# First down product in blocks of 512 tokens, and the second layer's weight combinations formed one product later

## The chip, the core and the metric

The kernel runs on one core of a Trainium2 chip. The metric is the device time of one execution in microseconds (us), compared as medians of runs on the same chip.

## What is computed

Attention with 32 packed queries per head (batch 8, 8 heads, 576 positions, head size 64) feeds two layers of the same shape (4608 tokens, model width 512, inner width 2048):

```python
p_packed = sm_attn(p, k, v)
x = sm_attn(q, p_packed, p_packed)        # then tokens x 512
h = x @ w_in;  y = (h * cos(h)) @ w_out                 # first layer
h = y @ w_in2; out = where(h >= 1, h, where(h <= -1, 0, (h + 1)**2 / 4)) @ w_out2
```

## The kernel before

All matmuls are float32 products in three terms: each operand is split into a rounded part and a remainder (`split`: one ScalarE copy at L67, one subtraction at L68), and `TERMS` names the three pairs that are multiplied. The weights arrive as 64-bit floats; `convert` rebuilds 32-bit values from their two words (L132 on ScalarE, then L134, L135, L138, L139 and L142 on VectorE).

The program has four stages, one after the other:

- **Front**: attention for batch n beside the first up product. `up(n, hf, fp)` is one item: 12 matmuls of 288 columns (L616), a copy `u` out of PSUM (L623 or L625) and a store of 288 KB to the scratch tensor `h1T`. There are 128 items, and beside each the streams of generators (`load`, `wt`, `wo`, `frm`, `mat`, `att`) are advanced by one step. The stream `wo` converts and splits `w_out` in 16 slices over the last 32 items (`cut_w_out`).
- **First down product** (`run_down1`): 16 blocks of 288 tokens, 8 items each. An item loads 288 KB of `h1T`, forms h*cos(h) (`act_a`: L789 and L790; `act_b`: L797 and L798), splits it into a tile `r1` (`part`), and multiplies it with `w_out` in 24 matmuls of 288 columns (L824). Loads run 7 items ahead in 8 buffers; `r1` has 4 buffers.
- **Second up product** (`run_up2`): 8 batches, 4 pairs of slices each, seven products (`ORDER_UP`) of 12 matmuls per pair (L745), since this layer multiplies 2 x 2 blocks with seven products in place of eight.
- **Second down product** (`run_down2`): again seven products per batch (L928).

The seven products need sums and differences of the weight blocks. `combine` forms them in units, as the stream `wt`: a unit loads 1 MB (two loads at L545), converts it, forms four combinations (L570 to L573), splits them, and stores seven pieces of 256 KB (L552) to `su` (for the up product, 8 units) or `sd` (for the down product, 8 units). The tiles of `su` and `sd` are read back by the loads at L668. A unit has one raw tile; its second half `hl` receives the split parts and must be stored before the next pair is written to it.

Instructions stand in a fixed order on each engine and each engine takes them in that order. The order was set by a scheduler when the program was built, from the order of the code and from what each instruction needs; memory that a pool takes over from a closed pool makes its first writers wait for the last readers. Before the change, the 8 units of `su` start in the middle of the front, in the pool `late` on the right side of memory; the pool of `r1` is opened on the same side after `late` is closed.

Of the kernel before, what the change touches and what calls it, by code (L numbers as in the profile page):

```python
# [9 lines left out]
F32 = mybir.dt.float32  # L10
# [17 lines left out]
def body(ctx: ExitStack, tc: tile.TileContext, q, k, v, p, w_in, w_out, w_in2, w_out2, out):  # L28
# [25 lines left out]
    h1T = dram.tile([NFT // 2, 128, NT // HB, 2, HB], F32, name="h1T")  # L54
# [486 lines left out]
    def combine(units):  # L541
        def load(src):
            raw = prep[0].tile([128, 4, 256, 2], I32, tag="raw", name="raw")
            for x in range(2):
                nc.sync.dma_start(out=raw[:, 2 * x:2 * x + 2], in_=src(x))  # L545
            return raw

        held = []

        def store():  # L550
            for dst, x in held:
                nc.sync.dma_start(out=dst, in_=x)  # L552
            held.clear()

        units = list(units)
        raw = load(units[0][0])
        yield
        for u, (_, dst) in enumerate(units):

            a = prep[0].tile([128, 4, 256], F32, tag="pa", name="pa")  # L560
            convert(raw, a, last_act)
            store()
            yield
            s, hl = (
                raw[:, 2 * i:2 * i + 2].rearrange("p m c t -> p (m c t)") for i in range(2)
            )
            s = s.bitcast(F32).rearrange("p (k c) -> p k c", c=256)
            hl = hl.bitcast(F32R).rearrange("p (l n c) -> p l n c", l=2, n=2)
            tt = nc.vector.tensor_tensor
            tt(out=s[:, 0], in0=a[:, 1], in1=a[:, 3], op=ALU.add)  # L570
            tt(out=s[:, 2], in0=a[:, 0], in1=a[:, 1], op=ALU.subtract)
            tt(out=s[:, 1], in0=s[:, 0], in1=a[:, 0], op=ALU.subtract)
            tt(out=s[:, 3], in0=a[:, 2], in1=s[:, 1], op=ALU.subtract)  # L573
            yield
            for k, n in ((0, 2), (2, 1), (3, 2), (5, 2)):
                x = {0: a[:, 0:4:2], 2: a[:, 3:4], 3: s[:, :2], 5: s[:, 2:]}[k]
                with behind(last_act):
                    split(hl[:, 0, :n], hl[:, 1, :n], x, nc.vector)
# [26 lines left out]
    def up(n, hf, fp):  # L605
# [20 lines left out]
        late_store(h1T[fp, :, 2 * n + hf], u)  # L626
# [83 lines left out]
    def bank(x):  # L710
        return ps2.tile([128, 2, 512], F32, tag=x, name="ps" + x, bufs=2 if x == "Z" else 1)[:, :, :HB]
# [58 lines left out]

    def load_h1(i):
        if i < B * 16:
            t = dn1["g"].tile([128, 2, HB], F32, tag="g", name="h1")
            nc.sync.dma_start(out=t, in_=h1T[i % 8, :, i // 8])
            G1[i] = t

    def run_down1():
        po = pd.enter_context(tc.tile_pool(name="dn_o", bufs=3, reuse_waits="tile"))
# [4 lines left out]
        streams["wt"].append(combine(list(units_down())[:4]))  # L783

        def act_a(i):
            if i < B * 16:
                t = turns[i] = pt.tile([128, 2, HB], F32, tag="t", name="t")
                ki = t.bitcast(I32)
                nc.scalar.activation(out=ki, in_=G1[i], func=AF.Copy, scale=1 / (2 * PI), bias=0.25)  # L789
                nc.vector.scalar_tensor_tensor(  # L790
                    out=t, in0=G1[i], scalar=1 / (2 * PI), in1=ki, op0=ALU.mult, op1=ALU.subtract
                )

        def act_b(i):
            if i < B * 16:
# [4 lines left out]
        def part(i):  # L800
            if i < B * 16:
                r = parts[i] = dn1["r"].tile([128, 2, 2, HB], F32R, tag="r", name="r1")
                split(r[:, 0], r[:, 1], turns.pop(i), nc.vector)
# [6 lines left out]
        for i in range(B * 16):  # L810
            blk, c = divmod(i, 8)
            if c == 0:
                acc = [bank("Z") for _ in range(2)] if blk % 2 else [bank(x) for x in "XY"]
            load_h1(i + 7)
# [4 lines left out]
            for k in range(2):  # L819
                f = 2 * c + k  # L820
                for d in range(NDT):
                    ds = slice(d * 128, d * 128 + 128)
                    for n, (w, y) in enumerate(TERMS):
                        nc.tensor.matmul(  # L824
# [3 lines left out]
            if c == 7:  # L828
                for j in range(2):
                    y = po.tile([128, 2, HB], F32, tag="o", name="o1")  # L830
# [4 lines left out]
                    late_store(  # L835
                        yT[j * 256:j * 256 + 256, blk * HB:blk * HB + HB].rearrange("(j p) t -> p j t", p=128), y
# [3 lines left out]
            if i % 4 == 2:  # L840
                step("wt")
            if i == 13 * 8:
                drain("wt")
                for o in ORDER_UP[:6]:
                    load_su(0, o)
# [6 lines left out]
    def run_up2():  # L852
# [12 lines left out]
        streams["wt"].append(combine(list(units_down())[4:]))  # L865
        last = None
        for p in range(B):
            for f in range(0, 8, 2):
# [4 lines left out]
                for o in ORDER_UP[:6]:  # L873
                    product_up(p, f, o, st)
                    if o[0] == "X":
# [113 lines left out]
    for i, (n, hf, fp) in enumerate(items):  # L989
# [9 lines left out]
        if i == n_first + 1:  # L999
# [4 lines left out]
            prep[:] = late  # L1004
            streams["wt"].append(combine(units_up()))
# [6 lines left out]
        if n == B - 1 and hf and fp == 0:  # L1012
# [73 lines left out]
```

## Time and profile before

| | |
|---|---|
| median of 3 runs | 1780.81 us (1777.97 to 1781.54) |
| the profiled execution | 1794.1 us, its span 1792.2 us |
| TensorE busy (PE) | 1582.3 us, 88% of the span |
| VectorE busy (DVE) | 1222.4 us, 68% |
| ScalarE busy (ACT) | 944.7 us, 53% |
| GpSimd busy (POOL) | 231.0 us, 13% |
| mean granted TensorE clock | 0.928 of full speed |
| moved by DMA | 333.24 MB, mean 186 GB/s |

The span runs from the first to the last instruction. TensorE is busy for most of it, but the shares differ by stage: in two stretches it is far from full, the front (0 to about 515 us) and the end of the front (515 to 603 us).

### The profile page before, as it was taken

The numbers are of one execution on the slowest core, as the hardware profiler recorded it, in microseconds if no ns is written. First come the engines' busy times: TensorE is split into PE (matmuls) and PEld (weight loads), VectorE is DVE, ScalarE is ACT, GpSimd is POOL, SyncE is SP. The second block draws the span as 40 slices with busy tenths as digits, with TensorE's granted clock in tenths as the row PEclk, the third lists the DMA queues.
The fourth block names the chain that finished last, engine by engine and source line by source line (L and its number), as shares of the span: only waits on it lengthen the run. The fifth ranks groups of instructions, "written<-read, shape, count | busy, mean of one in ns | idle before, by whom it ended". The sixth has DMA issues, their size and how long they took to land.

```text
span 1792.2 us, 28398 instructions
## 1 busy us (share of the span) xinstructions
PE 1582.3 (88%) x10846; PEld 1521.1 (85%) x10846; DVE 1222.4 (68%) x1787; ACT 944.7 (53%) x1530; POOL 231.0 (13%) x154
## 2 busy tenths in 40 slices
PE   9579988988830598999999999899999899999998
PEld 7459876878730598999999999889999899999998
DVE  6873345658763688887677467886666587777774
ACT  4353444545432466676666456667667444444443
POOL 0221001222000001000000213444442000000000
PEclk7779988989875799999999999999999999999999
DMA  7666889998785375554344555543334964444430
GB/s 254 162 184 211 242 295 278 303 300 300 267 281 178 99 214 160 182 164 119 108 120 117 200 200 191 177 159 132 131 133 178 396 198 133 133 133 133 133 107 34
DMA packets 177994, 333.24 MB, mean 186 GB/s; under 512 B 16576, under 2 KB 70848, under 8 KB 174272
## 3 DMA queue, kind: packets, MB, share of 16 engines
q1 hardware_dynamic: 123584, 237.02, 43.1%
q10 hardware_dynamic: 54272, 94.39, 14.1%
q8 instruction: 85, 1.39, 0.3%
q14 instruction: 53, 0.43, 0.1%
HBM read 190.84 MB, written 136.31 MB: 183 GB/s over the span
## 4 chain that ended last, share of the span: by engine, by line
PE 62%; DMA 19%; DVE 12%; issue 3%; ACT 3%; SPq 1%; ACTq 0%; DVEq 0%
PE psZ L928 9%; PE psZ L824 8%; PE hps L616 7%; PE psZ L745 6%; PE psY L928 5%; PE psX L928 5%; PE psY L745 4%; PE psX L745 4%; PE psX L824 4%; PE psY L824 4%; DMA sd<-raw 3%; DMA su<-raw 3%; DMA raw<-in_moe_w_in 3%; DMA raw<-in_moe_w_out 2%; PE psA L279 2%
## 5 line engine op out<-in xcount | busy, mean ns | idle before, releaser
L616 PE MATMUL hps<-at,m 128*128 128x288 f32 x1536 | 251.7, 321 | 33.9 <-ACT u L625 22.4
L616 PEld LDWEIGHTS hps<-at,m 128*128 128x128 f32 x1536 | 231.7, 206 | 48.1 <-ACT u L625 26.0
L67 ACT ACTIVATE r<-g 128x576 fp32r<-128x576 f32 x224 | 153.5, 686 | 180.7 <-PE psZ L928 71.6
L68 DVE TENSOR_TENSOR r<-g,r 128x576 fp32r<-128x576 f32 x224 | 166.3, 754 | 69.3 <-ACT r L67 69.1
L824 PE MATMUL psZ<-r,wo 128*128 128x288 f32 x1536 | 207.9, 296 | 4.4 <-DVE r L68 2.2
L824 PEld LDWEIGHTS psZ<-r,wo 128*128 128x128 f32 x1536 | 205.6, 188 | 6.0 <-DVE r L68 3.3
L824 PE MATMUL psX<-r,wo 128*128 128x288 f32 x768 | 126.2, 300 | 90.5 <-ACT r L67 87.6
L824 PEld LDWEIGHTS psX<-r,wo 128*128 128x128 f32 x768 | 111.4, 191 | 91.4 <-ACT r L67 87.9
L928 PE MATMUL psZ<-r,sw 128*128 128x288 f32 x1152 | 158.2, 296 | 1.6 <-DVE o L723 0.9
L928 PEld LDWEIGHTS psZ<-r,sw 128*128 128x128 f32 x1152 | 155.0, 188 | 2.0 <-issue 1.1
L731 DVE SCALAR_TENSOR_TENSOR t<-hh,t 128x576 f32<-128x576 f32 x128 | 117.6, 921 | 42.0 <-ACT t L730 41.5
L68 DVE TENSOR_TENSOR r<-t,r 128x576 fp32r<-128x576 f32 x128 | 99.1, 777 | 58.6 <-ACT r L67 58.4
L729 ACT ACTIVATE t<-hh,half 128x576 f32<-128x576 f32 x128 | 98.5, 772 | 57.2 <-DVE hh L723 46.5
L824 PE MATMUL psY<-r,wo 128*128 128x288 f32 x768 | 125.5, 299 | 0.0
L67 ACT ACTIVATE r<-t 128x576 fp32r<-128x576 f32 x128 | 86.9, 681 | 66.2 <-PE psZ L824 32.5
L68 POOL TENSOR_TENSOR ty<-td,ty 128x576 fp32r<-128x576 f32 x32 | 53.8, 1687 | 523.0 <-ACT ty L67 523.0
L745 PE MATMUL psZ<-ty,sw 128*128 128x288 f32 x768 | 112.8, 297 | 7.2 <-DVE hh L723 6.9
L928 PE MATMUL psX<-r,sm 128*128 128x288 f32 x768 | 108.2, 301 | 10.0 <-ACT r L67 9.8
L928 PEld LDWEIGHTS psX<-r,sm 128*128 128x128 f32 x768 | 106.0, 193 | 10.6 <-ACT r L67 10.1
L745 PEld LDWEIGHTS psZ<-ty,sw 128*128 128x128 f32 x768 | 105.6, 188 | 8.5 <-DVE hh L723 8.0
L824 PEld LDWEIGHTS psY<-r,wo 128*128 128x128 f32 x768 | 111.5, 191 | 0.0
L797 ACT ACTIVATE t<-t,halfpi 128x576 f32<-128x576 f32 x128 | 97.5, 767 | 14.1 <-DVE t L790 13.9
(160 smaller groups left out, 2820.0 us busy)
## 6 DMA issues: line engine op xcount, KB each, us to landing
h1T<-u ACTq DMA_DIRECT2D x128, 288.0 KB, 4.2
h<-h1T SPq DMA_DIRECT2D x128, 288.0 KB, 2.9
gT<-t ACTq DMA_DIRECT2D x128, 288.0 KB, 2.1
g<-gT SPq DMA_DIRECT2D x128, 288.0 KB, 3.2
raw<-in_moe_w_in SPq DMA_DIRECT2D x32, 512.0 KB, 5.7
raw<-in_moe_w_out SPq DMA_DIRECT2D x32, 512.0 KB, 5.4
su<-raw SPq DMA_DIRECT2D x56, 256.0 KB, 3.4
sd<-raw SPq DMA_DIRECT2D x56, 256.0 KB, 2.9
```

Source lines behind the costliest of these rows:

```text
L67: nc.scalar.activation(out=hi, in_=src, func=AF.Copy)
L68: (eng or nc.gpsimd).tensor_tensor(out=lo, in0=src, in1=hi.bitcast(F32), op=ALU.subtract)
L279: nc.tensor.matmul(out=pp[:, s * 64:s * 64 + 64], lhsT=ve[:, s * 128:s * 128 + 128], rhs=e[:, pos * 64:pos * 64 + 64], start=(c == 0), sto ...
L616: nc.tensor.matmul(out=hps[:, j, :HB], lhsT=m[:, w, G, cs], rhs=x[:, G, y], start=(G == 0 and i == 0), stop=(G == 1 and i == 2),)
L729: nc.scalar.activation(out=t, in_=h, func=AF.Relu, scale=0.5, bias=half)
L731: nc.vector.scalar_tensor_tensor(out=t, in0=h, scalar=1.0, in1=t, op0=ALU.max, op1=ALU.min)
L745: nc.tensor.matmul(out=ps[:, i], lhsT=s[:, d, w, cs], rhs=t[:, d, y], start=first and d == n == 0, stop=d == 1 and n == 2, skip_group_chec ...
L797: nc.scalar.activation(out=t, in_=t, func=AF.Sin, scale=2 * PI, bias=halfpi)
L824: nc.tensor.matmul(out=acc[d // 2][:, d % 2], lhsT=wo[f // 4, w][:, f % 4, ds], rhs=r[:, y, k], start=f == n == 0, stop=f == NFT - 1 and n ...
L928: nc.tensor.matmul(out=ps[:, j], lhsT=s[:, f % 4, w, j * 128:j * 128 + 128], rhs=r[:, y, k], start=first and f == n == 0, stop=f == 7 and ...
```

## The change

The first down product works in 9 blocks of 512 tokens: an item loads 512 KB, and its 24 matmuls have 512 columns; 72 items in place of 128. `h1T` is laid out so that a row of tokens is contiguous, so each store of `u` goes out in two pieces of 1152 bytes per partition in place of one of 2304. Its buffers are fewer and larger: 4 for the loads (3 items ahead in place of 7), 2 for `r1`, 2 for the output. The 8 units of `su` are advanced in the first down product, one step per item, and no longer in the front; all 8 units of `sd` are advanced in the second up product, three steps per pair in place of two. Split parts alternate between the raw tile and a new tile `pl`, so the wait for a store is for the one before the last. Six loads of `su` are wrapped in `issue_after` a matmul.

```diff
-    h1T = dram.tile([NFT // 2, 128, NT // HB, 2, HB], F32, name="h1T")
+    h1T = dram.tile([NFT // 2, 128, 2, NT], F32, name="h1T")
...
-            hl = hl.bitcast(F32R).rearrange("p (l n c) -> p l n c", l=2, n=2)
+            hls = [hl.bitcast(F32R).rearrange("p (l n c) -> p l n c", l=2, n=2),
+                   prep[0].tile([128, 2, 2, 256], F32R, tag="pl", name="pl")]
...
-            for k, n in ((0, 2), (2, 1), (3, 2), (5, 2)):
+            for j, (k, n) in enumerate(((0, 2), (2, 1), (3, 2), (5, 2))):
+                hl = hls[j % 2]
...
-        late_store(h1T[fp, :, 2 * n + hf], u)
+        t0 = n * S + hf * HB
+        late_store(h1T[fp, :, :, t0:t0 + HB], u)
...
+    n_items = NT // 512 * 8
...
-            t = dn1["g"].tile([128, 2, HB], F32, tag="g", name="h1")
-            nc.sync.dma_start(out=t, in_=h1T[i % 8, :, i // 8])
+            t = dn1["g"].tile([128, 2, 512], F32, tag="g", name="h1")
+            nc.sync.dma_start(out=t, in_=h1T[i % 8][:, :, i // 8 * 512:i // 8 * 512 + 512])
...
-        streams["wt"].append(combine(list(units_down())[:4]))
+        streams["wt"].append(combine(units_up()))
+        last_act.clear()
...
-            load_h1(i + 7)
+            load_h1(i + 3)
...
-            if i % 4 == 2:
+            if True:
                 step("wt")
-            if i == 13 * 8:
+            if i == 7 * 8:
                 drain("wt")
-                for o in ORDER_UP[:6]:
-                    load_su(0, o)
+                with tc.issue_after(mm.ins):
+                    for o in ORDER_UP[:6]:
+                        load_su(0, o)
...
-        streams["wt"].append(combine(list(units_down())[4:]))
+        streams["wt"].append(combine(units_down()))
...
-                    if o[0] == "X":
+                    if o in ("X1", "X2", "Y5"):
                         step("wt")
...
-            prep[:] = late
-            streams["wt"].append(combine(units_up()))
...
-            dn1["g"] = pd.enter_context(tc.tile_pool(name="dn_g", bufs=8, reuse_waits="tile", side="right"))
-            dn1["r"] = pd.enter_context(tc.tile_pool(name="dn_r", bufs=4, reuse_waits="tile", side="right"))
-            for j in range(7):
+            dn1["g"] = pd.enter_context(tc.tile_pool(name="dn_g", bufs=4, reuse_waits="tile", side="right"))
+            dn1["r"] = pd.enter_context(tc.tile_pool(name="dn_r", bufs=2, reuse_waits="tile", side="right"))
+            for j in range(3):
                 load_h1(j)
```

How the order on the engines moves is shown at two places. The first is VectorE's queue at the end of the front. Before, from the last slice of `w_out` (`wo`) to the subtractions of the first tiles `r_...` of the first down product; two whole units (`pa`, `raw`) stand between them, of which the second is the block from L134 to L68:

```order
L68 TENSOR_TENSOR wo<-w_4548,wo 128x512
...
L68 TENSOR_TENSOR raw<-raw 128x512 x2
L134 TENSOR_SCALAR pa<-raw 128x1024
L135 SCALAR_TENSOR_TENSOR pa<-raw,pa 128x1024
L138 TENSOR_SCALAR raw<-pa 128x1024
L139 SCALAR_TENSOR_TENSOR raw<-raw 128x1024
L142 TENSOR_TENSOR pa<-pa,raw 128x1024
...
L68 TENSOR_TENSOR raw<-raw 128x512 x2
L68 TENSOR_TENSOR r_4764<-t,r_4764 128x576
L68 TENSOR_TENSOR r_4771<-t,r_4771 128x576
```

After the change, the same queue from the last slice of `w_out` to the first tile `r_4524`:

```order
L68 TENSOR_TENSOR wo<-w_4316,wo 128x512
L134 TENSOR_SCALAR pa<-raw 128x1024
L135 SCALAR_TENSOR_TENSOR pa<-raw,pa 128x1024
L796 SCALAR_TENSOR_TENSOR t<-h_4361,t 128x1024
L138 TENSOR_SCALAR raw<-pa 128x1024
L796 SCALAR_TENSOR_TENSOR t<-h_4363,t 128x1024
L139 SCALAR_TENSOR_TENSOR raw<-raw 128x1024
L804 TENSOR_TENSOR t<-h_4361,t 128x1024
L796 SCALAR_TENSOR_TENSOR t<-h_4365,t 128x1024
L142 TENSOR_TENSOR pa<-pa,raw 128x1024
L796 SCALAR_TENSOR_TENSOR t<-h_4529,t 128x1024
L804 TENSOR_TENSOR t<-h_4363,t 128x1024
```

The next row is the subtraction of `r_4524`. In place of two whole units, the conversion of one unit (the fourth) and seven operations of the first items now stand ahead of the first `r` tile; three units have gone before, and four follow in the product.

The second place is SyncE's queue, which issues the loads, at the start of the first down product after the change. `h_...` are the loads of items 0 to 6 and on, `sm` the loads of `su` (L671) that `issue_after` encloses in the code:

```order
L552 DMA su<-pl 128x2x256 x2
L545 DMA raw<-in_moe_w_in 128x2x512 x2
L779 DMA h_4361<-h1T 128x2x512
...
L779 DMA h_4682<-h1T 128x2x512
L671 DMA sm<-su 128x2048
L552 DMA su<-raw 128x2x256 x2
...
L545 DMA raw<-in_moe_w_in 128x2x512
L671 DMA sm<-su 128x2048 x5
L779 DMA h_4795<-h1T 128x2x512
```

The stores of the third unit and the raw loads of the fourth stand ahead of the first item's load, and the six loads of `su` stand around the loads of items 8 to 10, not at item 56 where the code has them: `issue_after` binds instructions of the matmul's own engine, and these are issued by SyncE. Before, the same six loads stood among the loads of `w_out` at the end of the front.

## Rows read from the trace of the kernel before

**Rows 1.** The page: busy tenths and granted clock in 40 slices of 44.8 us.

```profile
PE   9579988988830598999999999899999899999998
PEclk7779988989875799999999999999999999999999
```

**Rows 2.** TensorE's waits, 602 to 1013 us: total, times, longest.

```profile
PE psX L824 <- ACT r L67: 87.6, 1, 87.6
```

**Rows 3.** Timeline at the end of the front: start, us, instructions, idle before.

```profile
511.74 3.54 PE L616 MATMUL hps<-at,m 128*128 128x288 f32 x24 [0.23 <-ACT u L625]
516.87 0.63 ACT L67 ACTIVATE wo<-w 128x512 fp32r<-128x512 f32 x1 [1.96 <-DVE w L142]
...
540.71 0.63 ACT L67 ACTIVATE wo<-w 128x512 fp32r<-128x512 f32 x1 [2.24 <-DVE w L142]
541.51 1.21 SPq L545 DMA_DIRECT2D raw<-in_moe_w_in  x2
549.89 1.10 ACT L132 ACTIVATE raw<-raw 128x1024 f32<-128x1024 f32 x1 [8.56 <-DMA raw<-in_moe_w_in]
...
576.92 1.21 SPq L545 DMA_DIRECT2D raw<-in_moe_w_in  x2
583.20 1.10 ACT L132 ACTIVATE raw<-raw 128x1024 f32<-128x1024 f32 x1 [9.95 <-DMA raw<-in_moe_w_in]
...
602.17 2.40 ACT L67 ACTIVATE r<-t 128x576 fp32r<-128x576 f32 x4
```

**Rows 4.** Chain that ended last, 330 to 545 us: its pieces on units' transfers.

```profile
370.48 6.68 DMA su<-raw
...
383.87 7.84 DMA raw<-in_moe_w_in
...
425.97 5.88 DMA su<-raw
...
432.58 8.77 DMA raw<-in_moe_w_in
...
474.45 8.64 DMA su<-raw
```

**Rows 5.** Windows: busy us of PE, PEld, DVE, ACT, POOL (instructions); clock, DMA share, GB/s.

```profile
400.00:500.00 100.00, 81.76 (x513) 77.74 (x513) 79.94 (x123) 47.55 (x78) 14.74 (x9) 0.89 0.85 286
...
542.00:603.00 61.00, 0.11 (x1) 0.11 (x1) 22.87 (x36) 14.02 (x21) 0.00 (x0) 0.50 0.45 144
```

**Rows 6.** TensorE's timeline: runs of matmuls of 288 and of 512 columns.

```profile
360.88 0.86 PE L426 MATMUL psD<-wi,mt 128*128 128x512 f32 x3
361.58 1.49 PE L616 MATMUL hps<-at,m 128*128 128x288 f32 x10
...
631.42 25.76 PE L824 MATMUL psZ<-r,wo 128*128 128x288 f32 x192
657.02 0.96 PE L824 MATMUL psX<-r,wo 128*128 128x288 f32 x6
```

**Rows 7.** TensorE's timeline: first matmuls of the two middle products.

```profile
602.89 0.61 PE L824 MATMUL psX<-r,wo 128*128 128x288 f32 x1 [87.62 <-ACT r L67]
...
1026.47 1.77 PE L745 MATMUL psX<-ty,sm 128*128 128x288 f32 x12
```

**Rows 8.** Groups by shape: count, busy, mean ns of one, idle before.

```profile
L135 DVE SCALAR_TENSOR_TENSOR pa<-raw,pa 128x1024 int32<-128x1024 int32 x16 | 20.8, 1300 | 0.1
L142 DVE TENSOR_TENSOR pa<-pa,raw 128x1024 f32<-128x1024 f32 x16 | 20.7, 1291 | 0.1
```

**Rows 9.** TensorE's timeline in the second up product: all four stalls beside units.

```profile
1083.13 3.14 PE L745 MATMUL psY<-ty,sm 128*128 128x288 f32 x12 [1.97 <-DVE hh L723]
1121.48 1.87 PE L745 MATMUL psX<-ty,sw 128*128 128x288 f32 x12 [1.38 <-ACT p L718]
1132.82 1.86 PE L745 MATMUL psZ<-ty,sw 128*128 128x288 f32 x12 [3.07 <-DVE hh L723]
1137.80 3.19 PE L745 MATMUL psY<-ty,sm 128*128 128x288 f32 x12 [3.13 <-DVE hh L723]
```

**Rows 10.** DMA issues: count, KB each, median us to landing.

```profile
h1T<-u ACTq DMA_DIRECT2D x128, 288.0 KB, 4.2
h<-h1T SPq DMA_DIRECT2D x128, 288.0 KB, 2.9
yT<-o ACTq DMA_DIRECT2D x32, 288.0 KB, 2.9
sm<-su SPq DMA_DIRECT2D x6, 1024.0 KB, 7.6
```

More of the change, by code (lines that the diff above doesn't have):

```diff
@@ L708, in load_y, with bank @@
         tile_of("Z4", diff(b21, t2, t2))
-    def bank(x):
-        return ps2.tile([128, 2, 512], F32, tag=x, name="ps" + x, bufs=2 if x == "Z" else 1)[:, :, :HB]
+    def bank(x, n=HB):
+        return ps2.tile([128, 2, 512], F32, tag=x, name="ps" + x, bufs=2 if x == "Z" else 1)[:, :, :n]
     def wtile(pool, tag, bufs):
@@ L769, in body @@
     G1 = {}
+    n_items = NT // 512 * 8
     def load_h1(i):
-        if i < B * 16:
-            t = dn1["g"].tile([128, 2, HB], F32, tag="g", name="h1")
-            nc.sync.dma_start(out=t, in_=h1T[i % 8, :, i // 8])
+        if i < n_items:
+            t = dn1["g"].tile([128, 2, 512], F32, tag="g", name="h1")
+            nc.sync.dma_start(out=t, in_=h1T[i % 8][:, :, i // 8 * 512:i // 8 * 512 + 512])
             G1[i] = t
     def run_down1():
-        po = pd.enter_context(tc.tile_pool(name="dn_o", bufs=3, reuse_waits="tile"))
+        po = pd.enter_context(tc.tile_pool(name="dn_o", bufs=2, reuse_waits="tile"))
         pt = pd.enter_context(tc.tile_pool(name="dn_t", bufs=4, reuse_waits="tile"))
@@ L782, in run_down1 @@
         prep[:] = [pd.enter_context(tc.tile_pool(name="prep1", bufs=1, reuse_waits="tile"))]
-        streams["wt"].append(combine(list(units_down())[:4]))
+        streams["wt"].append(combine(units_up()))
+        last_act.clear()
         def act_a(i):
-            if i < B * 16:
-                t = turns[i] = pt.tile([128, 2, HB], F32, tag="t", name="t")
+            if i < n_items:
+                t = turns[i] = pt.tile([128, 2, 512], F32, tag="t", name="t")
                 ki = t.bitcast(I32)
@@ L794, in act_b @@
         def act_b(i):
-            if i < B * 16:
+            if i < n_items:
                 t = turns[i]
@@ L800, in part @@
         def part(i):
-            if i < B * 16:
-                r = parts[i] = dn1["r"].tile([128, 2, 2, HB], F32R, tag="r", name="r1")
+            if i < n_items:
+                r = parts[i] = dn1["r"].tile([128, 2, 2, 512], F32R, tag="r", name="r1")
                 split(r[:, 0], r[:, 1], turns.pop(i), nc.vector)
@@ L809, in run_down1 @@
         part(0)
-        for i in range(B * 16):
+        for i in range(n_items):
             blk, c = divmod(i, 8)
             if c == 0:
-                acc = [bank("Z") for _ in range(2)] if blk % 2 else [bank(x) for x in "XY"]
-            load_h1(i + 7)
+                acc = [bank("Z", 512) for _ in range(2)] if blk % 2 else [bank(x, 512) for x in "XY"]
+            load_h1(i + 3)
             part(i + 1)
@@ L823, in run_down1 @@
                     for n, (w, y) in enumerate(TERMS):
-                        nc.tensor.matmul(
+                        mm = nc.tensor.matmul(
                             out=acc[d // 2][:, d % 2], lhsT=wo[f // 4, w][:, f % 4, ds], rhs=r[:, y, k],
@@ L829, in run_down1 @@
                 for j in range(2):
-                    y = po.tile([128, 2, HB], F32, tag="o", name="o1")
+                    y = po.tile([128, 2, 512], F32, tag="o", name="o1")
                     if j:
@@ L835, in run_down1 @@
                     late_store(
-                        yT[j * 256:j * 256 + 256, blk * HB:blk * HB + HB].rearrange("(j p) t -> p j t", p=128), y
+                        yT[j * 256:j * 256 + 256, blk * 512:blk * 512 + 512].rearrange("(j p) t -> p j t", p=128), y
                     )
```

## The prediction

> **What bounds the kernel now.** I read the page first. TensorE's row of slices [rows 1] shows a front that is mostly full, a hole at its end, and products that fill nearly everything from the fifteenth slice on. In the hole, the twelfth to fourteenth slices, the digits are 3, 0, 5, and the granted clock falls to 0.5 of full speed, its lower level. The waits of TensorE in the first down product [rows 2] name it: one wait of 87.6 us for ScalarE's copy into `r`. The timeline [rows 3] shows what happens inside: the last matmuls of the front end at 515.3, slices of `w_out` are finished until 541.3, and then two units of `su` run alone, one after the other, with their loads issued at 541.51 and 576.92. Only at 602.17 does `r` get written, and the product starts at 602.89 [rows 7]. `r` comes after both because its pool takes over memory of the units' pool `late`. Elsewhere units lie beside matmuls; these two lie beside nothing.
>
> In the front itself, the chain of waits runs through units too: five transfers of units make up 37.8 us of it between 370 and 483 [rows 4]. VectorE is busy 80% and the DMA engines 85% there, while TensorE's 513 matmuls of that window, at the pace worked out next, would fit in 68 of its 100 us [rows 5]. After that, the first down product runs without gaps: it takes 1026.47 - 602.89 = 423.6 us [rows 7], and 192 matmuls take 657.02 - 631.42 = 25.6 us, 0.1333 us each [rows 6], so its 3072 matmuls are 409.6 us and 14.0 us are start and small waits. TensorE is the bound of everything from 603 us on.
>
> **The change part by part.** All terms are in us of the profiled execution (1794.1, a span of 1792.2); it lies 13.3 above the median of 1780.81, and I carry the sum over to that median as it is.
>
> *Front, until its last up matmul.* Before, five units and the load of a sixth lie ahead of this point; after, two units do, late in the front. What can be won is bounded by the 37.8 us of unit transfers on the chain. Not all of it comes back: when one piece leaves a chain, the next-latest takes over, here `h1T` stores and slices of `w_out`, and two units remain. I take 22, a little over half; ends 5 and 40. The two-piece stores of `h1T` I cost at nothing: stores of `yT` already go out in pieces of 1152 bytes and land in 2.9 us at the median, against 4.2 for those of `h1T` [rows 10].
>
> *From the last up matmul to the first down matmul.* Before: 87.6. After, VectorE's and ScalarE's queues hold these steps ahead of the first `r`. Six slices of `w_out` follow the last up copy, the first half done: between 516.87 and 540.71 four intervals of slices took 23.84 us, 5.96 each [rows 3], so five of them are 29.8. The third unit stands between them. Its VectorE time comes from the window with two units and eight tile operations of 576 columns: an operation of 1024 takes 1.29 [rows 8], so one of 576 about 0.73, and (22.87 - 5.8)/2 = 8.5 us [rows 5]; I cost it at nothing, since a slice has six VectorE operations of 512 columns, which at half the durations of [rows 8] are under 4 of its 5.96 us, and at 8.5 if that cover fails. Then the third unit's last store must land before the raw tile is loaded again (about 3 us, as the stores of `yT` [rows 10]), the load takes 8.4 or 6.3 from issue to L132 [rows 3], mean 7.3, and L132 itself 1.1. L132 of the fourth unit stands ahead of the first item on ScalarE, so this wait is paid in full. Then VectorE has eleven rows and the subtraction of `r`: ten at 1.29 and two at about half, 14.2. Sum 29.8 + 3 + 7.3 + 1.1 + 14.2 = 55.4, a gain of 32. If slices and load overlap better it is 45, with the third unit uncovered 64: gains of 43 and 24. The two units that ran alone are not gone; they lie beside matmuls now.
>
> *The product itself.* 1728 matmuls of 512 columns. The front has such matmuls in runs of three: from 360.88 to 361.58 three starts, 0.2333 each [rows 6]. 1728 x 0.2333 = 403.2, a gain of 6.4 over 409.6. Bounds by the 288-column row: if its price is proportional to columns, 0.237 each and no gain; if the 0.0133 above 288 columns at 2.4 GHz is a fixed price per matmul, 0.2267 each, 391.7, a gain of 17.9. I take the measured run of three.
>
> The Trainium skill ("TensorE: Matmul & The Clock Gate", section "Back-to-back issue gap") gives N/2.4 plus 2.5 ns as the spacing of single matmuls, by which 512 columns would be an estimate of 215.8 ns and the product 372.9 us. The trace does not agree for 288 columns, 133.3 ns against the formula's 122.5, so I do not use it for the sum.
>
> Does VectorE keep up? An item needs three operations of 1.29, 3.9 us, against 24 x 0.2333 = 5.6 on TensorE. The units stand in the queue one per six to seven items: 6.5 x 3.9 + 8.5 = 33.8 against 36.4 us. It fits, with little room. With two `r` buffers ScalarE's copy for item i+1 waits for the end of item i-1 and then has one item, 5.6 us, for copy and subtraction (about 2.4) and what stands between; that is enough, but an item that also carries a conversion has 2 to 3 us of slack, not more. The `issue_after` does nothing for the `su` loads, which SyncE issues: five 1 MB loads go out ahead of item 10's load. At 7.6 us per landing [rows 10] for one, and a lead of three items or 16.8 us, I expect a wait of 2 us once; the ends are 0 and 10.
>
> *Second up product.* Twice as many units. The four before made TensorE wait 1.97 + 1.38 + 3.07 + 3.13 = 9.6 us, and after two of these waits twelve matmuls took 3.14 and 3.19 in place of 1.77 [rows 7, 9], 3.0 more with the other two: 12.6, or 3.1 per unit. Four more units at that price are 12.6. The tile `pl` takes some waits for stores off ScalarE, so I take 9; ends 0 and 25. The eighth unit's stores stand ahead of the last batch but one, so the second down product does not wait for `sd`.
>
> Sum: -22 - 32 - 6.4 + 2 + 9 = -49. Profiled 1745, median **1732**.
>
> **The rivals.**
>
> *The front frees more.* If the DMA engines were its true bound (85% busy at 286 GB/s, [rows 5]), three units fewer move 9 MB less, some 31 us at that rate, and the rest of the chain shortens too: 40 and 43 in place of 22 and 32, so -78, 1702. Against it: TensorE and VectorE stand on that chain as well.
>
> *The front hardly moves.* Slices of `w_out` pace its last 32 items at about 6 us per slice or more, units or not; then 5 and 24, and 12.6 for the units later: -20, 1760. For it: slices are spread over those items and wait for their loads.
>
> *512 columns at full rate.* In an unbroken run the price above the columns could vanish: 512/2.4 GHz is 0.2133, 368.6 in all, 34.6 more, 1697. Against it stands the unbroken run of 288 columns, at 0.1333 and not 0.12. (By the formula of the Trainium skill's page above it would be 30 more.)
>
> *Slower than before: the loads starve the product.* Three items of lead in place of seven, with stores and 1 MB loads ahead in SyncE's queue, each of which waits for VectorE. If every item waits, the gain of 49 is gone from 49/72 = 0.68 us per item on; at 1.5 us it ends at 1840. A tile of this sort lands in 2.9 us [rows 10] against a lead of 16.8, which speaks against it.
>
> *The change does not do what it says*: true of `issue_after`, whose price is in the sum.
>
> **How the numbers follow.** Forecast as summed 0.55 (1715 to 1748), more freed 0.17, hardly moved 0.17, full rate 0.04, starved 0.05, and 0.02 for gains and losses that cancel. A change of under 0.2%, 3.6 us, cannot be told from none. All but the last two are faster: 0.93, within 0.02, slower 0.05. The range from 1700 to 1763 leaves out the starved case, the full-rate case, nearly half of the "more freed" case and a little at the top.
>
> **What would show it.** Right: TensorE's wait ahead of the first down matmul falls from 87.6 to 45 to 64 us; the last up matmul ends between 475 and 510; 192 of the new matmuls take 44.8 us; the down product takes 405 to 422; stalls beside units in the second up product come to 15 to 30 in all. Wrong: waits for `h` loads in the down product, matmuls there with gaps at every item, a second up product more than 25 us longer than before, or a front that ends no earlier than 513.

## The result and the profile after

The changed kernel takes 1735.16 us at the median of 4 runs (1732.49 to 1736.27), the kernel before 1780.62 (1777.97 to 1781.54): a ratio of 0.9745, interval 0.9728 to 0.9762, or 45.5 us less. The forecast was 1732. The profiled execution took 1735.4 us, a span of 1733.6, so it stands for the median; that of the kernel before lay 13.5 above its own.

TensorE's slices on the page of the changed kernel, 43.3 us each, and the clock granted in them:

```profile
PE   9579998998816999999999889899999799999998
PEclk7769998999867999999999899999999899999999
```

Against [rows 1] the hole is most of the twelfth slice and a part of the thirteenth. The 0.6 there is a mean that takes in busy time; inside the hole, from 505 to 533, the granted clock is 0.50 as before. TensorE's timeline answers [rows 3, 6, 7]: the last up matmuls, the first of the first down product, one uninterrupted run of 192, the first of the second up product and of the second down product.

```profile
481.62 1.85 PE L618 MATMUL hps<-at,m 128*128 128x288 f32 x12 [0.77 <-ACT u L627]
533.85 0.79 PE L830 MATMUL psX<-r,wo 128*128 128x512 f32 x1 [50.37 <-ACT r L67]
...
584.47 44.96 PE L830 MATMUL psZ<-r,wo 128*128 128x512 f32 x192
629.27 0.39 PE L830 MATMUL psX<-r,wo 128*128 128x512 f32 x1
...
954.57 1.76 PE L748 MATMUL psX<-ty,sm 128*128 128x288 f32 x12
...
1353.55 2.70 PE L935 MATMUL psX<-r,sm 128*128 128x288 f32 x19
```

The end of the front is the start of the first down matmul less its wait: 483.5, against 515.3. Reading such rows for every kernel gives the table to which all that follows refers. Each row of it is one profiled execution; the last column reaches to the end of the span. "Move" is the move of the combinations, "blocks" are those of 512 tokens.

| kernel | median us | front ends | wait | first down | second up | rest |
|---|---|---|---|---|---|---|
| before, profile of 1794.1 | 1780.6 | 515.3 | 87.6 | 423.6 | 384.1 | 381.6 |
| before again, 1781.55 | | 509.1 | 85.4 | 422.6 | 382.7 | 380.0 |
| changed | 1735.2 | 483.5 | 50.4 | 420.7 | 399.0 | 380.0 |
| blocks alone | 1798.0 | 514.8 | 94.5 | 420.0 | 387.5 | 380.6 |
| move alone | 1710.2 | 473.9 | 33.7 | 424.4 | 397.3 | 379.4 |
| move, h1T in two pieces | 1712.2 | 469.1 | 34.1 | 428.3 | 395.4 | 380.3 |
| changed, no `pl` | 1734.0 | 481.0 | 40.4 | 428.8 | 398.8 | 379.0 |
| changed, units held | 1705.6 | 474.0 | 26.5 | 426.5 | 400.1 | 380.9 |
| changed, `su` loads held | 1730.1 | 479.3 | 50.8 | 421.4 | 402.3 | 380.5 |
| move, units held | 1699.9 | 472.4 | 27.2 | 425.5 | 390.8 | 379.5 |
| the same, first load held | 1705.0 | 468.1 | 23.8 | 428.4 | 405.2 | 379.4 |
| the same, ten units and six | 1699.5 | 472.9 | 23.0 | 432.5 | 392.5 | 380.4 |
| move, held, GpSimd added | 1727.7 | 475.9 | 27.4 | 448.8 | 394.6 | 379.2 |
| the same, 4 columns | 1706.3 | 473.4 | 26.6 | 430.5 | 395.3 | 379.3 |

Where blocks are of 512 tokens, 24 matmuls of the second up product (3.2 us) lie ahead of the end of the first down product (25 and 26 without `pl` and with the units held), so that its own time is 3.2 less than in the table, and the second up product's 3.2 more. The kernels ran on several chips, on which the kernel before had medians of 1780.6 to 1785.8; where two kernels on different chips differ by about 5 us, their ratios to it are what counts.

What fills the wait of 50.4 us shows in the timelines of SyncE and ScalarE, which answer [rows 3]: loads of the units' raw tiles, the last slice of `w_out`, the fourth unit's conversion (L132), and the first `r`. The last two rows, of VectorE and TensorE, are the subtraction of the same `r` and the matmuls that wait for it.

```profile
410.99 1.27 SPq L545 DMA_DIRECT2D raw<-in_moe_w_in  x2
450.58 1.46 SPq L545 DMA_DIRECT2D raw<-in_moe_w_in  x2
485.47 0.56 SPq L545 DMA_DIRECT2D raw<-in_moe_w_in  x1
...
514.88 0.63 ACT L67 ACTIVATE wo<-w 128x512 fp32r<-128x512 f32 x1 [2.33 <-DVE w L142]
515.56 1.21 SPq L545 DMA_DIRECT2D raw<-in_moe_w_in  x2
523.82 1.10 ACT L132 ACTIVATE raw<-raw 128x1024 f32<-128x1024 f32 x1 [8.32 <-DMA raw<-in_moe_w_in]
...
532.75 1.04 ACT L67 ACTIVATE r<-t 128x1024 fp32r<-128x1024 f32 x1
...
536.51 1.22 DVE L68 TENSOR_TENSOR r<-t,r 128x1024 fp32r<-128x1024 f32 x1
...
537.79 2.50 PE L830 MATMUL psX<-r,wo 128*128 128x512 f32 x5 [2.72 <-DVE r L68]
```

Two units lie wholly in the front, the third beside the last slices, and ScalarE then waits 8.32 us for the fourth's load, as the forecast had it. In the second up product TensorE's timeline has 21 waits where the kernel before has eight (four of them are [rows 9]); the longest of them, the first being that for the product's first tiles:

```profile
964.84 3.25 PE L748 MATMUL psX<-ty,sm 128*128 128x288 f32 x12 [6.91 <-ACT p L721]
...
1019.40 1.87 PE L748 MATMUL psY<-ty,sm 128*128 128x288 f32 x12 [2.28 <-DVE hh L726]
...
1122.10 1.87 PE L748 MATMUL psY<-ty,sm 128*128 128x288 f32 x12 [2.56 <-DVE hh L726]
...
1219.73 2.89 PE L748 MATMUL psZ<-ty,sw 128*128 128x288 f32 x12 [3.22 <-DVE hh L726]
```

### The profile page after: what moved, and what is told of

It is laid out like the page before. It is cut to its first block, busy times and chain, and to the rows that moved or that the text cites. A ratio compares the mean times of both kernels' runs of the same rounds, so it can differ in the third digit from the quotient of the medians.

```text
span 1733.6 us, 25137 instructions
## 1 busy us (share of the span) xinstructions
PE 1566.0 (90%) x9502; PEld 1422.9 (82%) x9502; DVE 1211.8 (70%) x1612; ACT 913.7 (53%) x1355; POOL 232.2 (13%) x154
## 4 chain that ended last, share of the span: by engine, by line
PE 61%; DMA 17%; DVE 13%; issue 4%; ACT 3%; SPq 1%; ACTq 0%; POOL 0%; DVEq 0%; POOLq 0%
PE psZ L935 9%; PE psZ L830 8%; PE hps L618 8%; PE psY L935 6%; PE psX L935 5%; PE psX L830 5%; PE psY L830 5%; PE psZ L748 4%; DMA h1T<-u 3%; DMA raw<-in_moe_w_in 3%; DMA raw<-in_moe_w_out 3%; PE psY L748 3%; PE psX L748 2%; PE psA L279 2%; DVE t L734 2%
## 5 line engine op out<-in xcount | busy, mean ns | idle before, releaser
L618 PE MATMUL hps<-at,m 128*128 128x288 f32 x1536 | 238.8, 311 | 20.3 <-ACT u L627 15.7
L68 DVE TENSOR_TENSOR r<-g,r 128x576 fp32r<-128x576 f32 x224 | 166.6, 755 | 69.3 <-ACT r L67 69.3
L830 PE MATMUL psX<-r,wo 128*128 128x512 f32 x480 | 135.3, 404 | 58.3 <-ACT r L67 50.4
L830 PE MATMUL psZ<-r,wo 128*128 128x512 f32 x768 | 179.8, 395 | 0.0
L830 PEld LDWEIGHTS psZ<-r,wo 128*128 128x128 f32 x768 | 144.2, 188 | 35.0
L830 PEld LDWEIGHTS psX<-r,wo 128*128 128x128 f32 x480 | 91.3, 192 | 82.9 <-ACT r L67 50.8
L734 DVE SCALAR_TENSOR_TENSOR t<-hh,t 128x576 f32<-128x576 f32 x128 | 122.3, 960 | 36.8 <-ACT t L733 36.7
L830 PE MATMUL psY<-r,wo 128*128 128x512 f32 x480 | 133.2, 399 | 0.0
L68 DVE TENSOR_TENSOR r<-t,r 128x1024 fp32r<-128x1024 f32 x72 | 88.9, 1235 | 47.1 <-ACT r L67 47.1
L68 POOL TENSOR_TENSOR ty<-td,ty 128x576 fp32r<-128x576 f32 x32 | 55.6, 1743 | 449.8 <-ACT ty L67 449.7
L935 PEld LDWEIGHTS psX<-r,sm 128*128 128x128 f32 x768 | 105.8, 193 | 10.5 <-ACT r L67 10.0
L830 PEld LDWEIGHTS psY<-r,wo 128*128 128x128 f32 x480 | 91.4, 190 | 22.2
L804 DVE TENSOR_TENSOR t<-h,t 128x1024 f32<-128x1024 f32 x72 | 87.9, 1220 | 28.6 <-ACT t L803 28.4
L803 ACT ACTIVATE t<-t,halfpi 128x1024 f32<-128x1024 f32 x72 | 82.4, 1145 | 43.8 <-DVE t L796 43.8
```

Source lines behind the costliest of these rows:

```text
L68: (eng or nc.gpsimd).tensor_tensor(out=lo, in0=src, in1=hi.bitcast(F32), op=ALU.subtract)
L618: nc.tensor.matmul(out=hps[:, j, :HB], lhsT=m[:, w, G, cs], rhs=x[:, G, y], start=(G == 0 and i == 0), stop=(G == 1 and i == 2),)
L734: nc.vector.scalar_tensor_tensor(out=t, in0=h, scalar=1.0, in1=t, op0=ALU.max, op1=ALU.min)
L803: nc.scalar.activation(out=t, in_=t, func=AF.Sin, scale=2 * PI, bias=halfpi)
L804: nc.vector.tensor_tensor(out=t, in0=G1.pop(i), in1=t, op=ALU.mult)
L830: mm = nc.tensor.matmul(out=acc[d // 2][:, d % 2], lhsT=wo[f // 4, w][:, f % 4, ds], rhs=r[:, y, k], start=f == n == 0, stop=f == NFT - 1 ...
```

## The experiments

**The kernel before, once more.** No edit.

> The kernel before once more, unchanged. In its first profile it took 1794.1 us, 13.3 over its median of 1780.81. Theory: the 13 us lie in one stage that varies from run to run, the front with its many transfers, so a profile of about 1781 shows the last up matmul some 13 us earlier than 515.3 (near 502) and the same 87.6 us wait and the same products behind it. Then the change won about 19 us in the front, close to the forecast of 22, and the trace of 1794.1 over-counted it. Rival A: the 13 us lie in the wait ahead of the first down product (near 75 in place of 87.6): then it was the wait that won less. Rival B: they are spread over all stages in proportion (0.7% of each), as a lower clock would give: front 512, wait 87, down product 420.5, up product 381. Expected time 1781, within 0.3%.

TensorE's timeline in that execution:

```profile
505.62 3.46 PE L616 MATMUL hps<-at,m 128*128 128x288 f32 x24 [1.35 <-ACT u L625]
594.45 0.61 PE L824 MATMUL psX<-r,wo 128*128 128x288 f32 x1 [85.36 <-ACT r L67]
...
1017.00 1.76 PE L745 MATMUL psX<-ty,sm 128*128 128x288 f32 x12
...
1399.73 2.70 PE L928 MATMUL psX<-r,sm 128*128 128x288 f32 x19
```

Of the 12.5 us by which the spans differ, 6.2 lie in the front, 2.2 in the wait and 4.0 in the three products. Neither the theory (all in the front) nor rival A holds; it is nearest to rival B, with half of it in the front. Against this execution, which stands at the median, the change won 25.6 in the front and 35.0 in the wait.

**Blocks alone, and the move alone.** The first keeps every hunk of the diff on blocks and layout, and `pl`, and puts the combinations back; the second does the reverse:

```diff
-        streams["wt"].append(combine(list(units_down())[:4]))
+        streams["wt"].append(combine(units_up()))
+        last_act.clear()
...
-            if i % 4 == 2:
+            if i % 2 == 1:
                 step("wt")
-            if i == 13 * 8:
+            if i == 14 * 8:
                 drain("wt")
...
-        streams["wt"].append(combine(list(units_down())[4:]))
+        streams["wt"].append(combine(units_down()))
...
-                    if o[0] == "X":
+                    if o in ("X1", "X2", "Y5"):
...
-            prep[:] = late
-            streams["wt"].append(combine(units_up()))
```

> Only the blocks of 512 tokens; all combinations stand where they stood before. Theory (the gain is that of the moved units): the wait ahead of the first down matmul stays near 88 us, the last up matmul ends within 5 us of where it ends before, the down product takes 410 to 424, so 1770 to 1781, ratio 0.994 to 1.000. Rival (the larger blocks bring most of it, by fewer and longer instructions and stores in the front): 1750 or less, ratio 0.983 or lower.

> Only the combinations moved: blocks of 288 tokens as before. Theory: TensorE's wait ahead of the first down matmul falls to 45 to 60, the last up matmul ends 15 to 32 us earlier, the down product stays at 418 to 432 (256 operations per engine of 576 columns in place of 72 of 1024 leave less room beside the units), the second up product is 10 to 20 longer; in all 1735 to 1750, ratio 0.974 to 0.983. Rival (512 columns are needed for the units to fit beside the product): TensorE waits in the down product for the splits, more than 20 us of it, and the time is 1760 or more, ratio over 0.988.

Blocks alone make the kernel slower: 1798.03 us (1794.47 to 1799.21, 6 runs), ratio 1.0082 (1.0053 to 1.0110). The move alone takes 1710.16 us (1703.98 to 1715.55), ratio 0.9582 (0.9530 to 0.9634), 25 us less than with the blocks. Both times lie outside the ranges of theory and rival, and both expectations erred to the side of the blocks. TensorE's timeline with the move alone:

```profile
470.38 3.52 PE L616 MATMUL hps<-at,m 128*128 128x288 f32 x19
507.65 0.61 PE L825 MATMUL psX<-r,wo 128*128 128x288 f32 x1 [33.74 <-ACT r L67]
...
932.06 1.77 PE L745 MATMUL psX<-ty,sm 128*128 128x288 f32 x12
```

The first down product took 424.4 us with all eight units beside it, 1.8 more than before with four: blocks of 512 were not needed for the units to fit. With blocks alone, against the second execution of before, the wait grows by 9.1 and the second up product by 4.8 (8.0 with the 24 matmuls); the front ends 5.7 later, but the two executions of the kernel before differ there by 6.2. On top of the move, the blocks cost 9.6 in the front and 16.6 in the wait. The next kernels ask why.

**The layout of h1T.** The move alone, with the changed layout of the intermediate:

```diff
-    h1T = dram.tile([NFT // 2, 128, NT // HB, 2, HB], F32, name="h1T")
+    h1T = dram.tile([NFT // 2, 128, 2, NT], F32, name="h1T")
...
-        late_store(h1T[fp, :, 2 * n + hf], u)
+        t0 = n * S + hf * HB
+        late_store(h1T[fp, :, :, t0:t0 + HB], u)
```

> Only the combinations moved, blocks of 288, but with the layout of the intermediate that blocks of 512 need: each partition's store is two pieces of 1152 bytes in place of one of 2304, and each load too. Forecast by the working on record: stores in two pieces cost nothing, so 1705 to 1716, as without this layout (1710.2), and a front that ends within 3 us of 473.9. Rival (more and smaller packets cost the front, where the DMA engines are 80 to 90% busy): the last up matmul ends 5 to 12 us later and the time is 1716 to 1725.

1712.22 us (1709.04 to 1716.52), ratio 0.9604 (0.9575 to 0.9633), and a front that ends at 469.1, 4.8 earlier. The instructions of TensorE, VectorE and SyncE stand in the same order in both kernels; the stores landed in 3.7 us at the median, against 3.2. The stores in two pieces cost nothing that these runs can tell. That step of the forecast holds.

**The units held.** In the changed kernel, and in that with the move alone, the combinations are put behind ScalarE's first copy into `r`:

```diff
-        streams["wt"].append(combine(units_up()))
...
-        part(0)
+        last_act[:] = [part(0)]
+        streams["wt"].append(combine(units_up()))
```

> The changed kernel (blocks of 512 tokens), with the combinations of the second up product held behind ScalarE's first copy into r, so that none of them stands in the front or at its end. In the changed kernel two units and a part of the next two stand there; its last up matmul ends at 483.5 and TensorE then waits 50.4 us. In the kernel with the units moved and blocks of 288 no unit stands ahead of the last up copy, and these were 473.9 and 33.7. Theory (the place of the units, not the size of the blocks, makes this difference): the last up matmul ends within 5 us of 474, the wait falls to 32 to 42, and with all eight units beside the product the time is 1710 to 1722. Rival (the larger blocks cost it, by stores in smaller pieces in the front and longer operations ahead of the first r): the front ends at 480 or later, and the time stays at 1725 or more.

> Only the combinations moved, blocks of 288, and these held behind ScalarE's first copy into r. There the first unit's conversion and splits stand between the last slices of w_out and the first r: from 486 to 499 VectorE and ScalarE work on both by turns and TensorE waits 33.7 us. Theory (the first unit delays the slices and the first r): without it the wait falls to 20 to 30, time 1698 to 1707. Rival (the slices of w_out and their loads alone pace that stretch, the unit lies in their gaps): the wait stays at 31 to 36 and the time within 4 us of 1710.

The changed kernel falls to 1705.58 us (1702.60 to 1709.81), below the expectation; its front ends at 474.0 and its wait is 26.5 us. The move alone falls to 1699.90 (1697.17 to 1701.22), ratio 0.9536 (0.9508 to 0.9563), the first of two that take the least time. Both theories hold: the place of the units is what the larger blocks cost, all but 5.7 us (1705.6 against 1699.9, on one chip). The two profiled executions, the slowest of one kernel and the fastest of the other, are 12.6 apart, and 9.3 of that lie in the second up product. With 288 tokens SyncE issues no unit's load before 478; with 512 they go out from 411 on (above). Why the order came out so differently was not tried.

**The first load held.** In the kernel with move and held units, SyncE and ScalarE show the first unit's loads ahead of the last load of `w_out`, and what waits for that:

```profile
478.37 1.28 SPq L545 DMA_DIRECT2D raw<-in_moe_w_in  x2
479.74 0.55 SPq L518 DMA_DIRECT2D raw<-in_moe_w_out  x1
487.00 0.65 ACT L132 ACTIVATE raw<-raw 128x512 f32<-128x512 f32 x1 [3.96 <-DMA raw<-in_moe_w_out]
```

```diff
-            nc.sync.dma_start(out=t, in_=h1T[i % 8, :, i // 8])
+            dn1["last"] = nc.sync.dma_start(out=t, in_=h1T[i % 8, :, i // 8]).ins
...
         streams["wt"].append(combine(units_up()))
+        with tc.issue_after(dn1["last"]):
+            step("wt")
```

> As the kernel with the units moved, blocks of 288 and the units behind the first copy into r, and also the first unit's two loads held behind the first seven loads of h. In that kernel these two loads (512 KB each) stand ahead of the last load of w_out in SyncE's queue, and ScalarE then waits 3.96 us for that slice. Theory: the slice comes 3 to 4 us earlier and the wait ahead of the first down matmul falls from 27.4 to 23 to 25, so 1695 to 1698 in place of 1699.9. Rival (the DMA engines are busy there in any case, the slice's own load is late): no difference, within 2 us of 1700.

The wait fell to 23.8 as expected, but the time is 1705.03 us (1700.76 to 1706.65), outside both ranges; against the kernel before, each on its own chip, the ratios are 0.9567 (0.9531 to 0.9603) and 0.9536 (0.9508 to 0.9563), so that it is not shown to be slower, only not faster. In the profiled execution the second up product took 405.2 in place of 390.8. The edit also changed the order of the instructions on every engine from there on. In that product TensorE waits 34.1 us in place of 23.0, and VectorE is busy 312.1 in place of 301.4 with the same operations: what it lost lies in operations that run while GpSimd works, of which the last section tells. Why this order costs more of them stays open, and so does what else is in the 14 us.

**Ten units and six.** On top of that, two units of the second down product move to beside the first:

```diff
-        streams["wt"].append(combine(units_up()))
+        streams["wt"].append(combine(list(units_up()) + list(units_down())[:2]))
...
-            if i % 2 == 1:
+            if i % 3 != 0:
                 step("wt")
...
-        streams["wt"].append(combine(units_down()))
+        streams["wt"].append(combine(list(units_down())[2:]))
```

> As the kernel with the first unit's loads held, with two of the eight units of the second down product moved from beside the second up product to beside the first down product, ten there and six here. From the profiles so far, four more units made the first down product at most 3 us longer (425 in place of 422) and the second up product 8 to 16 longer (391 to 399 in place of 383), 0.5 and 2 to 4 us each. Theory (a unit is cheaper beside the down product): 3 to 7 us faster than with eight and eight, 1690 to 1695. Rival (VectorE, 80 to 90% busy beside that product already, becomes the bound there): TensorE waits for the splits in many items and the time is 1700 or more.

1699.52 us (1694.96 to 1705.50), 5.5 less than without, but no better than the kernel with held units, and between the ranges of theory and rival. The first down product grew by 4.1, the second up product shrank by 12.7; runs scatter too much to settle the price of one unit.

**Two smaller edits of the changed kernel.** One leaves out `pl`, so that each split waits for the store before it; the other puts the `su` loads behind the load of `h1T` that is the last one at that point of the program, the sixtieth of 72 (they go out at 833 to 836 us in place of 545 to 558):

```diff
-            hls = [hl.bitcast(F32R).rearrange("p (l n c) -> p l n c", l=2, n=2),
-                   prep[0].tile([128, 2, 2, 256], F32R, tag="pl", name="pl")]
+            hl = hl.bitcast(F32R).rearrange("p (l n c) -> p l n c", l=2, n=2)
```

```diff
-                with tc.issue_after(mm.ins):
+                with tc.issue_after(dn1["last"]):
```

> The changed kernel without the second buffer of split tiles for the combinations: each split waits for the store of the one before. Theory: the waits stand in the queues of ScalarE and VectorE ahead of the splits of the products; four stores of about 3 us per unit in place of two, so stalls beside units grow in the second up product from about 25 to 30 to 45 us, and the time is 4 to 15 us above the changed kernel's 1735 (1739 to 1750). Rival (the waits fall into slack, or other waits take their place): within 3 us of 1735.

> The changed kernel with the six loads of su really held until the last load of an intermediate tile is issued; as changed they go out earlier, ahead of items of the product in SyncE's queue. The working on record gave these loads 2 us of wait, with ends of 0 and 10. In the changed kernel's profile TensorE waits for no tile of h there. Theory: no wait is to be had back, so the time is within 4 us of 1735, or up to 5 above it if the first su tiles now come late for the second up product. Rival (the loads delay VectorE's or ScalarE's work by what they take of the DMA engines): 3 to 8 us faster.

Without `pl`: 1734.02 us (1729.87 to 1737.27), no difference; the rival holds. The waits of the second up product, without its first, are 24.1 us, not the 30 to 45 of the theory; the order at the end of the front changed too, with a wait 10.0 shorter and a first down product 8.1 longer. With the loads held: 1730.14 (1728.52 to 1736.23), 5.0 less, which is the rival's 3 to 8 and not the theory's 4; but the ratios, 0.9709 (0.9680 to 0.9738) and 0.9745 (0.9728 to 0.9762), overlap. The execution that was profiled is the slowest of its four and shows no gain: its front ends 4.2 earlier, ahead of the edit, and its second up product is 3.3 longer. Whether the loads cost anything stays open.

**GpSimd beside VectorE.** The kernel with move and held units, with operations added whose results nothing uses; then the same on 4 columns:

```diff
+                if i % 2:
+                    x = px.tile([128, 2, HB], F32, tag="x", name="x")
+                    nc.gpsimd.tensor_tensor(out=x, in0=G1[i], in1=G1[i], op=ALU.add)
```

> As the kernel with the units moved, blocks of 288 and the units behind the first copy into r (1699.9 us), with work added that no output needs: for every second of the 128 items of the first down product GpSimd adds a tile of h to itself, 576 columns, 64 operations of about 1.4 us. In the second up product, where GpSimd works too, operations of VectorE on 256 columns range from 0.41 to 1.65 us; in most of the first down product, where it does not, all take 0.42. Theory (VectorE's operations take longer while GpSimd works): the same spread appears beside the first down product, VectorE's work there grows by up to 64 x 1.2 = 77 us against some 64 of slack, and the product grows from 425 to 440 to 500. Rival (the spread in the second up product has another cause, GpSimd's work costs VectorE nothing): durations of 0.42 as before, the product within 4 us of 425.

> The control to the kernel with 64 added operations on GpSimd: the same 64 operations with the same waits and the same readers of h, each on 4 columns in place of 576. The order of instructions on VectorE, ScalarE and TensorE is the same in both, and the same as without them. Theory (the time for which GpSimd works is what counts): the product stays within 4 us of 425, the whole within 5 of 1699.9. Rival (the added readers hold up loads of h and so cost what the larger operations cost): as slow as the other kernel.

1727.68 us (1725.43 to 1729.84) against 1706.32 (1705.46 to 1706.77) for the control. First and second row: durations (shortest, median, longest in ns) of one of VectorE's operations in that product, with 576 columns added and with 4.

```profile
L802 DVE TENSOR_TENSOR t<-h,t x128: 737/751/1972, 500.8 to 931.2; 128x576 f32<-128x576 f32 x128
```

```profile
L802 DVE TENSOR_TENSOR t<-h,t x128: 736/752/761, 497.5 to 909.6; 128x576 f32<-128x576 f32 x128
```

And TensorE's waits within the product with 576 columns, in total, times, longest:

```profile
PE psX L829 <- DVE r L68: 12.7, 8, 4.1
PE psZ L829 <- DVE r L68: 7.1, 5, 2.6
```

The product takes 448.8 us against 430.5 in the control and 425.5 without; VectorE is busy 380.9 of the 425 us from 500 on, against 343.4. The instructions of TensorE, VectorE and SyncE stand in the same order in all three, and the added operations take 1.48 us at the median with 576 columns, 0.51 with 4. The theory holds. The control's product is 5.0 longer than without any addition and its time 6.4 longer than 1699.9, each about one more than expected; whether the added waits cost this, or the other chip and the spread of executions, is not shown.

## Why the prediction was right

The mechanism was right: the units at the end of the front were what TensorE waited for, and beside matmuls they cost less. That the total came within 3.5 us was luck in part: front and wait together won 15 us more than forecast against the profiled execution, the second up product lost 9 more, and the 13 us by which that execution lay above the median, carried over as they were, more than took up the rest. Term by term, against the execution of before on which the sum was made, and against the one at the median:

- *Front*: forecast -22; measured -31.8 and -25.6. Mis-sized, inside its ends of 5 and 40. The last up matmul ended at 483.5, inside the 475 to 510 given. Three units fewer there gave more than half of [rows 4] back; the two that remained cost about 9.5 more (474.0 with the units held), and all of them together 35.1, most of those 37.8.
- *Wait*: forecast -32, that is 55.4; measured 50.4, -37.2 and -35.0, inside 45 to 64. The steps came in the order listed, at other sizes: 31.4 us to the last slice with the third unit beside it (29.8 forecast, the unit at nothing), 0.7 to the load's issue (3), 8.3 to L132 (7.3), 1.1 for it, and 8.9 from there to the first matmul (14.2). The last was misread: 14.2 counts up to the end of VectorE's subtraction of `r`, but the first matmul waits for ScalarE's copy alone, in [rows 2] already. The subtraction ended at 537.7, and the 2.7 us for which TensorE waited for it lie in the product.
- *Product*: forecast -6.4. 192 matmuls took 629.27 - 584.47 = 44.80 us, the 44.8 of the forecast. Less the 3.2 of the second up product it took 417.5: -6.1 and -5.1. Inside 405 to 422. Of the two edits that the forecast put together, though, the blocks cost time: their 6 us here are less than what they cost at the front's end. The forecast had no term for that, since it took the units' place as given.
- *`su` loads*: forecast +2; measured 0. After them ScalarE waited once for a tile of `h`, 2.46 us at 576.91, and no matmul waited with it. What TensorE waited for in the product was VectorE's subtraction of `r`, 7.9 us in five waits: the 2.7 above, and 5.2 in four others, the longest 3.2.
- *Second up product*: forecast +9 (ends 0 and 25); with the 3.2, measured +18.1 and +19.5. Against the execution at the median this is the term that was off by most. Its waits beside units came as forecast, 24.5 us in 20 waits against 13.7 before (the four of [rows 9], one of 3.70 at 1187.65 that these leave out, and two of 0.4 together), inside the 15 to 30 given. What it lacked: `pl`, credited with 3.6 us, brings nothing; the product's first wait grew from 3.50 to 6.91; and the rest, some 4 us, lies for the most part in runs of matmuls that go slowly behind a wait (twelve in 2.93 at 971.80 and in 3.05 at 1032.96, where 1.76 is the pace; the granted clock is 0.52 from 962 to 975 and 0.57 from 1032 to 1036).
- *From profile to median*: forecast as it is. The sum of -58.6 in the profiled executions is -45.5 in the medians; 13 us of it belong to one slower execution of before. Against the execution at the median, the 22 and 32 forecast for front and wait lie only 3.6 and 3.0 below what was won; the wait itself, forecast as 55.4, is off by 5.0 against either.

No rival came about. "The front frees more" asked for 40 and 43, against 31.8 and 37.2 at most; "512 columns at full rate" fell with the 44.80; "starved" with the absence of waits for `h` on TensorE; of "hardly moves", the 12.6 for the units in the second up product was nearer than the 9, still below the 18.1, and the front did move.

## What to carry to other kernels

A change of two parts is forecast part by part, each alone too: here one part won 71 us alone and the other lost 16, and the sum looked like one gain. Work taken off a critical stretch is to be held explicitly behind the first instruction that ends the stretch; here that was worth 30 us more than moving it in program order with blocks of 512, and 10 with blocks of 288. Before a sum is made against one profiled execution, see how far this lies from the median and in which stages.

## What the runs showed of the hardware

That VectorE slows down beside GpSimd was not expected. In the changed kernel GpSimd forms the first tiles of the second up product at 646 to 655 us, within the first down product. VectorE's and GpSimd's timelines there, with TensorE's wait for the `r` of the second row, and one VectorE row of the unit after it:

```profile
646.18 1.44 POOL L68 TENSOR_TENSOR ty<-yb,ty 128x576 fp32r<-128x576 f32 x1
646.40 2.30 DVE L68 TENSOR_TENSOR r<-t,r 128x1024 fp32r<-128x1024 f32 x1 [1.76 <-ACT r L67]
647.58 2.41 POOL L699 TENSOR_TENSOR td<-yb,td 128x576 f32<-128x576 f32 x1
648.63 1.64 DVE L571 TENSOR_TENSOR raw<-pa 128x256 f32<-128x256 f32 x1
648.76 1.43 PE L830 MATMUL psX<-r,wo 128*128 128x512 f32 x5 [1.25 <-DVE r L68]
650.19 0.41 DVE L572 TENSOR_TENSOR raw<-pa 128x256 f32<-128x256 f32 x1
```

The same kind of operation took 1.64 us beside GpSimd and 0.41 when GpSimd had just ended; one of 1024 columns took 2.30 in place of 1.22. Each lost about 1.1 to 1.2 us, and TensorE waited 1.25 us for that `r`; it waited 3.20 for the next one, at 657.82. In the second up product GpSimd works for much longer, 105.8 of the 280 us from 955 to 1235. VectorE's groups there, 955 to 1235 us (count, busy us, mean ns of one, idle before):

```profile
L734 DVE SCALAR_TENSOR_TENSOR t<-hh,t 128x576 f32<-128x576 f32 x82 | 82.1, 1007 | 13.1 <-ACT t L733 13.1
L726 DVE TENSOR_TENSOR hh<-psZ,q 128x576 f32<-128x576 f32 x21 | 15.7, 749 | 5.6 <-PE psZ L748 5.4
...
L139 DVE SCALAR_TENSOR_TENSOR raw<-raw 128x1024 f32<-128x1024 uint32 x8 | 13.8, 1721 | 0.1
L138 DVE TENSOR_SCALAR raw<-pa 128x1024 int32<-128x1024 int32 x8 | 9.0, 1125 | 0.0
L571 DVE TENSOR_TENSOR raw<-pa 128x256 f32<-128x256 f32 x8 | 7.9, 990 | 0.0
```

An operation with an input from PSUM (L726) keeps its 0.75 us; one of the same size that has both from SBUF (L734) takes 1.01 at the mean. Of its 82 operations, the 54 during which the trace has none of GpSimd's took 0.75 at the mean and 0.76 at most, the other 28 took 1.50 at the mean. The units' thirteen groups sum to 95.8 us, 12.0 per unit. In the kernel before the same thirteen operations took 9.2 us in the second of the two units that ran alone, with GpSimd idle; the forecast's 8.5 was a little low. How much of TensorE's waits in the second up product comes from this is not shown, but the kernels with added work on GpSimd show that such work can cost TensorE 18 us in one product. The Trainium skill ("SBUF — State Buffer", section "SBUF: two separate sides") says that the two engines share a pair of ports, and that of a GpSimd operation that reads SBUF and a VectorE operation with two inputs from SBUF, or a GpSimd operation and a VectorE operation in a mode that uses two ports, whichever starts first holds the pair for its whole length. These runs agree for two inputs: 1.50 us for L734 beside GpSimd against 0.75, and no change for L726, which has one of its two from PSUM. That L138, with one input, is lengthened as well (1.13 at the mean in place of 0.69) would be the case of two ports; no run here shows which mode it used.
